# One written list of steps for all five engines of an attention and MLP kernel, in another order

## The chip, the cores and the metric

The kernel runs on one core of a Trainium2 chip. A core has a matrix engine (TensorE, PE in the profile, with its weight loads shown as PEld), a vector engine (VectorE, DVE), a scalar engine (ScalarE, ACT), a general engine (GpSimd, POOL) and an engine that issues transfers (SyncE, SP). Each takes its instructions from a queue of its own, in order, and they wait for one another by semaphores. The data lies in the chip's main memory, in an on-chip memory of 128 partitions (SBUF), and, for the results of matmuls, in eight banks of PSUM, 512 float32 values per partition each.

The metric is the device time of one execution in microseconds (us). Four executions of the kernel before gave 324.56 to 325.36, median 325.13 us.

## The reference

The kernel joins two layers. The first is causal attention over a sliding window of 128 positions, with a linear bias that falls with the distance (ALiBi), for 8 batches and 8 heads, 576 positions, head size 64. Its output, reordered to 4608 tokens of 512 values, goes through an MLP whose activation is h * sigmoid(beta * h), with one beta for each of the 2048 hidden values.

```python
def _attn_ref(q, k, v):
    scores = scale * np.matmul(q, k.transpose(0, 1, 3, 2))
    slopes = 2.0 ** (-8.0 * (np.arange(H, dtype=np.float32) + 1) / H)
    bias = slopes[:, None, None] * (-np.abs(rel).astype(np.float32))[None, :, :]
    mask = (rel >= 0) & (rel < window)
    scores = np.where(mask, scores + bias[None], -1000000000.0)
    ...
    return np.matmul(attn, v).astype(np.float32)

def _moe_ref(x, w_in, w_out, beta):
    h = x @ w_in
    g = h * (1.0 / (1.0 + np.exp(-beta * h)))
    return (g @ w_out).astype(np.float32)
...
    x = np.ascontiguousarray(attn_out.transpose(0, 2, 1, 3)).reshape(B * S, H * D)
    return _moe_ref(x=x, **moe_kwargs)
```

All inputs and the output are float32. The kernel computes with bfloat16 operands and float32 sums.

## The kernel before

**The MLP.** The 4608 tokens are nine groups of 512 (group 0 to 8). For a group, `Hm` (line 557) makes 16 up-projection steps, one for each 128 of the hidden values. A step is four matmuls of 128x128 weights against 512 tokens (four, because the 512 inputs of a token are four times 128), into one PSUM bank. ACT takes the tanh of the bank (line 564), DVE makes from tanh and bank the gated value and writes it to `gT` (line 565); with that the bank is free. `OS` (line 588) then makes the output of each 128 tokens: 16 matmuls into one bank, issued in four steps of four, a copy to SBUF (line 598, ACT; one half of the last by line 596, DVE), and `store` (line 606). The output steps of a group mostly run after the up-projection steps of that group, some of them between those of the next. The input of the up-projection lies transposed in `XT`, a ring of 1536 tokens (three groups).

**The attention.** 576 positions are four blocks of 128 and one of 64. The batches go two ways.

Batches 0 and 1 run by pairs of heads. `get_pair` loads q or k of a pair for 512 positions (SyncE), `cast_pair` (line 235, POOL) turns them to bfloat16, `TP` (line 287) transposes them on TensorE and copies them into `qkT` (k by DVE, line 289, q by ACT, line 293), `SP_` (line 335) makes the scores, with a bias by a matmul (line 324) for some, ACT takes the exponential (line 342), `PVP` (line 374) the output, `norm` (lines 358 and 359, DVE) divides by the sum, and `XP` (line 385) transposes the result on TensorE, from where it is copied to `XT`. The 64 last positions have steps of their own (`TT`, `SCT`, `PV`, `X`).

Batches 2 to 7 run by blocks. `get` (line 207, SyncE) loads 128 positions of q, k or v for all heads; `cast_qk` (lines 228 and 229, POOL) casts q and k into a staging buffer `bst`; `DT` (line 413) moves that transposed into `qkT`, by a DMA transpose that SyncE issues; `SC` (line 438) makes the scores for two pairs of heads at once, in the PSUM tiles `SS` and `ST` of two banks each, ACT takes the exponential (line 446), DVE multiplies by the falling factors (line 171 or 176), `PVB` (lines 492 and 495) makes the output of one block and normalises it on DVE (lines 499 and 500), into `xn`. `X` brings `xn` transposed into `XT`: for batches 2 and 3 by four matmuls against an identity (line 520) and a copy by ACT (line 523), for batches 4 to 7 by a DMA transpose on SyncE (line 512), which the constant `XDMA = 4` decides. v of batch 2 comes as q and k do, with a cast on POOL (line 243); v of batches 3 to 7 by `get_v` (line 250), a transfer by POOL's queue that casts on the way.

A token group needs the blocks of `XT` that it covers. Group 1 ends with block 3 of batch 1, group 2 with block 2 of batch 2, group 3 with block 2 of batch 3, and so on.

**The order.** The order on TensorE, SyncE and POOL is that of the program text. The opening (batch 0's attention and the first steps of group 0) is written out by hand, and there ACT and DVE follow the text too; later a scheduler orders these two. Group 0's steps are mixed by hand with batch 1's attention. From group 1 on, `spread` runs through a group's list of MLP steps and puts the attention steps of the batches to come between them, in proportion to the weights that `att` gives them, so that the blocks that group g+1 needs are in place when the steps of group g end. Loads, casts and transposes of the next batch stand in the same list (`jobs`). All loads of 32-bit data are issued by SyncE, W1 and W2 (lines 258 and 262) by POOL. W2 goes in four parts. The first transpose of batch 2 waits on purpose for the last of them:

```python
        if (b, sb) == (2, 0):
            after(r, w2[3])
```

The stores of groups 0 to 2 are issued by POOL, those after by ACT, the last two by SyncE. A few matmuls on zeros (`idle`, line 118, and `calm`) fill gaps in the opening.

**Buffers.** 14 for loads (`fst`), 4 for casts (`bst`), 10 for exponentials (`pt`), 4 for normalised blocks (`xn`), 2 for gated groups (`gT`), 3 for tanh (`sig`), 5 for outputs. The eight banks of PSUM are shared out by pools: two for `SS`, two for `hps`, two for transposes, which become `ST` later, and two for `SX`, which become `ops` and `h3`.

The functions that the change touches, with the line numbers of the profile:

Of the kernel before, what the change touches and what calls it, by code (L numbers as in the profile page):

```python
# [15 lines left out]
P = 128  # L16


@with_exitstack
def kernel(  # L20
# [18 lines left out]
    NQB = 5  # L39
# [44 lines left out]
    psum_c = ctx.enter_context(tc.tile_pool(name="psum_c", bufs=1, space=bass.MemoryType.PSUM))  # L84
    psum_h = ctx.enter_context(tc.tile_pool(name="psum_h", bufs=2, space=bass.MemoryType.PSUM))
    trans = ExitStack()
    psum_t = trans.enter_context(tc.tile_pool(side="right", name="psum_t", bufs=2, space=bass.MemoryType.PSUM))
    SS = psum_c.tile([P, 2, 512], F32, name="SS")
    psum_c.seal()
    opening = ExitStack()  # L90
    psum_x = opening.enter_context(tc.tile_pool(name="psum_x", bufs=1, space=bass.MemoryType.PSUM))
    SX = psum_x.tile([P, 2, 512], F32, name="SX")
    late, gates = {"tick": 0}, {}
    spans = [SS]

    def span():

        spans.append(spans.pop(0))
        return spans[-1]

    def obank(name, tag=None):
        if tag is None:
            late["n"] = late.get("n", 0) + 1
            tag = "ops" if late["n"] % 2 else "h3"
        return late["o"].tile([P, DM], F32, name=name, tag=tag)[:]

    def after(ins, other):
        tc.add_manual_dep(
            ins.ins, other.ins.name,
            mybir.DependencyInfo(mybir.DependencyClass.Sync, mybir.DependencyReason.DATA),  # L110
            reason="gate",
        )

    def idle(n):
        for _ in range(n):
            nc.tensor.matmul(
                SS[:, 0, :], lhsT=zeros[:, 0:P], rhs=zeros[:], start=True, stop=True,
                skip_group_check=True)  # L120

    def constants():
# [4 lines left out]
        idle(8)  # L127
# [35 lines left out]
    def falls_late(i):  # L163
        to, a, w = ((0, 0, P), (128, 0, 64), (192, 0, P), (320, 1, 64), (384, 1, P))[i]
        after(nc.vector.tensor_copy(
            out=falls[:, :, to : to + w], in_=fall[:, :, a, 0:w]), gates[1, 4])

    def factor(pt, m, p):

        if m:  # L170
            nc.vector.tensor_tensor(  # L171
                out=pt[:], in0=pt[:], in1=falls[:, 2 * p : 2 * p + 2], op=ALU.mult)
            return
# [16 lines left out]
    def betas():  # L190
        bps = psum_t.tile([P, NFF], F32, name="bps", tag="t")
# [703 lines left out]
```

The softmax here doesn't subtract the row's maximum and nothing guards it: scores larger than these inputs give would overflow.

## Time and profile before

| What | Before |
|---|---|
| median of four executions | 325.13 us |
| the profiled execution's own time | 325.27 us |
| its span, first to last instruction | 323.5 us |
| TensorE: busy, matmuls | 310.1 us (96%), 2256 |
| VectorE, ScalarE, GpSimd busy | 183.7, 194.0, 98.8 us |
| first up-projection matmul of group 0, 1, 2 | 19.27, 48.02, 93.65 us |
| the same of group 3 to 8 | 125.0, 157.7, 190.5, 221.8, 254.3, 284.5 us |
| read from and written to main memory | 36.71 and 9.44 MB |

A page of the profile shows one execution. "Busy" is the time in which an engine works on an instruction; matmuls overlap, and their ends are modelled, so TensorE's share is an upper bound. The slices cut the span in 40 equal parts and give the busy share of each in tenths, and the clock granted to TensorE. A group of instructions is one line of the program on one engine, with operation, tile, shape, number, busy time, mean duration, and the idle time of the engine just before them with what ended it. "L557" is line 557. The chain of waits goes back from the last instruction: at each step to whatever released it. "DMA qkT<-bst" in it is the transfer that fills `qkT` from `bst`. Names that end in q, such as SPq, are an engine's queue of instructions.

### The profile page before, as it was taken

What the parts mean: (1) busy time and instruction counts of PE and PEld (TensorE: products, weight loads), DVE (VectorE), ACT (ScalarE), POOL (GpSimd) and SP (SyncE); (2) the same over time, 40 slices, a digit from 0 to 9 for tenths busy, and PEclk for the clock granted to TensorE, in tenths of its full rate; (3) what the DMA queues carried; (4) which work ended last, traced back from release to release, by engine and by line L of the source; (5) the groups of instructions that cost most, each with busy time, mean ns of one, the idle gap of its engine ahead of it and who ended that gap; (6) DMA issues with size and microseconds to landing.
All of it is one profiled execution on the core that took longest, in us unless ns stands there. A gap on an engine that the chain in (4) does not pass through costs nothing.

```text
span 323.5 us, 5947 instructions
## 1 busy us (share of the span) xinstructions
PE 310.1 (96%) x2256; PEld 153.0 (47%) x2297; DVE 183.7 (57%) x346; ACT 194.0 (60%) x283; POOL 98.8 (31%) x154
## 2 busy tenths in 40 slices
PE   8889999999999999999999999999999999999995
PEld 3444554444545454544454445444544455444443
DVE  6778877542548753786278617752875176335500
ACT  6858887635558865685467645845675465346511
POOL 4864810332853445438036221340000000000000
PEclk9999999999999999999999999999999999999999
DMA  7999999999999999999999994993122112110021
GB/s 212 254 263 248 175 195 198 223 198 161 217 180 158 205 256 132 233 167 165 256 196 205 157 254 83 215 138 101 18 65 60 65 18 65 47 61 32 10 89 65
DMA packets 147565, 48.84 MB, mean 151 GB/s; under 512 B 135360, under 2 KB 143824, under 8 KB 147536
## 3 DMA queue, kind: packets, MB, share of 16 engines
q1 hardware_dynamic: 115712, 32.39, 56.1%
q0 software_dynamic: 28624, 10.29, 26.9%
q10 hardware_dynamic: 3200, 5.78, 5.0%
q8 instruction: 18, 0.29, 0.4%
q14 instruction: 11, 0.09, 0.1%
HBM read 36.71 MB, written 9.44 MB: 143 GB/s over the span
## 4 chain that ended last, share of the span: by engine, by line
PE 78%; DMA 11%; POOL 3%; DVE 2%; ACT 2%; issue 2%; SPq 1%; DVEq 0%; POOLq 0%
PE ops L588 25%; PE hps L557 24%; PE hpo L557 11%; PE oph L588 9%; DMA fst<-in_k_dram 5%; DMA qkT<-bst 3%; DMA fst<-in_q_dram 3%; PE SS L438 2%; PE ST L438 1%; PE SS L495 1%; POOL bst L235 1%; PE SS L492 1%; ACT pt L446 1%; DVE gT L565 1%; PE ST L492 1%
## 5 line engine op out<-in xcount | busy, mean ns | idle before, releaser
L588 PE MATMUL ops<-W,gT 128*128 128x512 bf16 (+1 forms) x448 | 107.6, 372 | 1.1 <-ACT osb L598 0.5
L565 DVE SCALAR_TENSOR_TENSOR gT<-sig,hps 128x512 bf16<-128x512 bf16 x100 | 67.6, 683 | 71.8 <-ACT sig L564 71.6
L557 PE MATMUL hps<-XT,W 128*128 128x512 bf16 x383 | 98.1, 379 | 1.4 <-issue 0.3
L564 ACT ACTIVATE sig<-hps,beta_h 128x512 bf16<-128x512 f32 x100 | 68.1, 690 | 34.7 <-PE hps L557 33.3
L588 PEld LDWEIGHTS <-gT 128*128 128x128 bf16 x592 | 55.6, 98 | 61.6 <-issue 1.9
L557 PEld LDWEIGHTS <-W 128*128 128x128 bf16 x576 | 52.8, 98 | 61.1 <-issue 3.7
L228 POOL CAST bst<-fst 128x512 bf16<-128x512 f32 (+1 forms) x32 | 21.0, 657 | 76.1 <-DMA fst<-in_q_dram 44.4
L557 PE MATMUL hpo<-XT,W 128*128 128x512 bf16 x164 | 42.8, 379 | 0.2
L564 ACT ACTIVATE sig<-hpo,beta_h 128x512 bf16<-128x512 f32 x42 | 29.0, 689 | 16.9 <-PE hpo L557 15.7
L565 DVE SCALAR_TENSOR_TENSOR gT<-sig,hpo 128x512 bf16<-128x512 bf16 x42 | 28.6, 681 | 10.9 <-ACT sig L564 10.7
L598 ACT ACTIVATE osb<-ops 128x512 f32<-128x512 f32 (+1 forms) x28 | 16.6, 595 | 25.5 <-PE ops L588 20.6
L446 ACT ACTIVATE pt<-SS 128x1024 bf16<-128x1024 f32 x24 | 24.5, 1019 | 11.4 <-PE SS L438 11.4
L588 PE MATMUL oph<-W,gT 128*128 128x512 bf16 x126 | 29.2, 379 | 0.1
L229 POOL CAST bst<-fst 128x512 bf16<-128x512 f32 (+1 forms) x32 | 21.7, 677 | 16.9 <-DMA fst<-in_k_dram 15.4
L176 DVE TENSOR_TENSOR pt<-pt,fall 128x1024 bf16<-128x1024 bf16 x24 | 17.0, 709 | 14.6 <-ACT pt L446 14.6
L446 ACT ACTIVATE pt<-ST 128x1024 bf16<-128x1024 f32 x24 | 24.5, 1022 | 0.0
L171 DVE TENSOR_TENSOR pt<-pt,falls 128x1024 bf16<-128x1024 bf16 x24 | 18.9, 793 | 9.6 <-ACT pt L446 9.6
L250 POOL DMA_DIRECT2D vs<-in_v_dram x25 | 21.3, 869 | 0.0
L598 ACT ACTIVATE osb<-oph 128x512 f32<-128x512 f32 x8 | 4.8, 597 | 21.1 <-PE oph L588 21.1
L495 PEld LDWEIGHTS <-pt 128*128 128x128 bf16 x240 | 14.8, 97 | 4.3
L243 POOL CAST vs<-fst 128x512 bf16<-128x512 f32 (+1 forms) x15 | 10.1, 673 | 16.2 <-DMA fst<-in_v_dram 16.2
L492 PEld LDWEIGHTS <-pt 128*128 128x128 bf16 x192 | 13.4, 97 | 2.8
(102 smaller groups left out, 253.3 us busy)
## 6 DMA issues: line engine op xcount, KB each, us to landing
fst<-in_k_dram SPq DMA_DIRECT2D x32, 256.0 KB, 5.8
fst<-in_q_dram SPq DMA_DIRECT2D x32, 256.0 KB, 5.7
out_dram<-osb ACTq DMA_DIRECT2D x22, 256.0 KB, 2.0
fst<-in_v_dram SPq DMA_DIRECT2D x12, 256.0 KB, 5.6
out_dram<-osb POOLq DMA_DIRECT2D x12, 256.0 KB, 5.4
vs<-in_v_dram POOLq DMA_DIRECT2D x20, 128.0 KB, 6.3
W<-in_moe_w_in_dram POOLq DMA_DIRECT2D x4, 512.0 KB, 7.9
W<-in_moe_w_out_dram POOLq DMA_DIRECT2D x4, 512.0 KB, 13.2
```

The lines of the kernel that those rows point to most:

```text
L171: nc.vector.tensor_tensor(out=pt[:], in0=pt[:], in1=falls[:, 2 * p : 2 * p + 2], op=ALU.mult)
L228: nc.gpsimd.tensor_copy(out=t[0:rows, 0], in_=fs.pop(("q", b, sb))[0:rows])
L229: return nc.gpsimd.tensor_copy(out=t[0:rows, 1], in_=fs.pop(("k", b, sb))[0:rows])
L250: return nc.gpsimd.dma_start(out=VS[b % 2][0:rows, sb, :, 0:D], in_=v[b, :, P * sb : P * sb + rows, :].rearrange("h p d -> p h d"))
L446: nc.scalar.activation(out=pt[:], in_=sps[:], func=ACTF.Exp, scale=qscale)
L492: nc.tensor.matmul(o, lhsT=weights(b, qb - 1, h, 1), rhs=vs[:, qb - 1, h, 0 : D + 1], start=True, stop=False, skip_group_check=True)
L495: nc.tensor.matmul(o, lhsT=weights(b, qb, h, 0), rhs=vs[:, qb, h, 0 : D + 1], start=qb == 0, stop=True, skip_group_check=True)
L557: nc.tensor.matmul(hps, lhsT=W1[:, c, bass.ts(j, P)], rhs=XT[:, c, c0 : c0 + TOKG], start=(c == 0), stop=(c == NDM - 1),)
L564: gates[g, j] = nc.scalar.activation(out=sig[:], in_=hps, func=ACTF.Tanh, scale=beta_h[:, j : j + 1])
L565: gates["gT"] = nc.vector.scalar_tensor_tensor(out=gts[g][:, j, :], in0=sig[:], scalar=1.0, in1=hps, op0=ALU.add, op1=ALU.mult)
L588: nc.tensor.matmul(ops_[:, cols], lhsT=gT[:, j, i * P : i * P + P], rhs=W2[:, j, cols], start=(j == 0), stop=(j == NFF - 1),)
L598: nc.scalar.mul(o, ops_[:, cols], 0.5)
```

## The change

The program text that made the order goes away: the hand-written opening, `spread`, `jobs`, `att`, `merged`. In its place stands one list, `PLAN`, of 1300 short words, and a loop that runs them in order. A word is a step, after the point the engine that it goes to where there is a choice (`p` POOL, `v` DVE, `a` ACT, `s` SyncE), and numbers. `H:2:5:7` is the up-projection step 5 of group 2 into bank 7, `a:2:5` its tanh, `d:2:5` its gate; `O:0:3:1:7` the second quarter of the output of rows 3 of group 0 in bank 7, `oc` its copy, `st` its store. `gq.s:2:1` loads q of batch 2, block 1; `cQ.v:2:1` casts it on DVE; `D:2:1` transposes the block into `qkT`; `S`, `E`, `M` are scores, exponential and factor of a pair of heads; `V`, `n`, `XD` output, normalisation and DMA transpose of a block. The order on all five engines, ACT and DVE included, is now that of the list.

What differs in the steps:

- Each function that issued work for several engines is cut into one function for each engine (`TP` and `TPC`, `SP_` and `EP`, `PVB` and `NB`, `Hm`, `HA` and `HD`, and so on).
- PSUM is one tile of eight banks, and each step names its bank. Scores are made for one pair of heads at a time.
- The 79 casts, all on POOL before, are 24 on POOL, 31 on DVE, 24 on ACT. Of the 35 full output copies 8 go to DVE. The copies of the first transposes go to either engine.
- Batches 2 and 3 lose the matmuls and the ACT copies of `X`: all blocks of batches 2 to 7 go by DMA transpose (`XD`, 30 steps).
- All loads of q, k and v other than `get_v` go by SyncE, in another order, W1 and W2 by POOL, W2's parts in the order 2, 0, 1, 3. The wait for the last part of W2 goes. The change's short description says at most eight transfers are in flight; no line of the diff states that, it is a property of the order.
- Output stores are spread over ACT, POOL and SyncE, and some stand later in the list.
- The last 128 rows of the output are two steps of half the width (`OL`), each with its own copy (`lc`) and store (`ls`); the second half's copy was on DVE before, both are on ACT now.

```diff
+PLAN = """
+q.s:0:0 q.s:0:2 const fr:3 fr:7 z:1:1 k.s:0:0 fr:0 cq.p:0:0 q.s:0:1 k.s:0:3 ones cq.v:0:2 ck.v:0:0
+fr:5 z:2:5 q.s:0:3 z:2:6 Rk:0:0:1 rk.a:0:0 Rq:0:0:7 cq.a:0:3 ck.a:0:3 q.s:1:0 k.s:0:2 k.s:0:1
+rq.v:0:0 fr:6 fr:4 cq.v:0:1 Rq:0:2:4 A:0:0:1:1 rq.a:0:2 EA:0:0 cq.p:1:0 gv.s:0:1 B:0:0:5:0 Rk:0:3:7
+Rq:0:3:0 ck.v:0:2 rq.v:0:3 ck.p:0:1 k.s:1:0 cv.p:0:1 EB:0:0 order rk.v:0:3 Rq:0:1:4 Rk:0:1:5
+rk.a:0:1 Rk:0:2:1 z:1:6 gv.s:0:0 gv.s:0:3 k.s:1:1 rq.v:0:1 rk.a:0:2 MB:0:0 A:0:1:6:1 ck.p:1:0
+cv.v:0:0 B:0:1:3:0 gv.s:0:2 EA:0:1 EB:0:1 A:0:3:0:1 B:0:2:6:1 w1:0 Rk:1:0:4 EA:0:3 EB:0:2 A:0:2:2:1
+VA:0:0:0 rk.v:1:0 B:0:3:5:1 nA:0:0 EA:0:2 Rq:1:0:0 cv.p:0:3 MB:0:1 VA:0:2:4 cv.v:0:2 ck.a:1:1
+rq.a:1:0 w1:1 VA:0:3:1 q.s:1:1 q.s:1:3 VB:0:0:2 nA:0:2 nB:0:0 k.s:1:2 VB:0:2:0 Rk:1:1:4 z:2:7 nB:0:2
+beta:3 pad k.s:1:3 EB:0:3 VA:0:1:5 B:1:0:6:0 rk.a:1:1 cq.a:1:3 EB:1:0 A:1:0:2:1 nA:0:1 nA:0:3
+VB:0:3:5 VB:0:1:4 XP:0:0:7 cq.p:1:1 w1:2 nB:0:1 nB:0:3 XP:0:2:6 ck.v:1:2 EA:1:0 Rq:1:3:4 Rq:1:1:3
...
+d:0:10 TT:0:1 tt.a:0 a:0:11 gk.s:2:0 VB:1:0:5 VB:1:2:7 nB:1:0 B:1:3:3:1 SCT:0:0 w2:2 nB:1:2 cv.v:0:4
...
+x.a:0:4 xc.v:1:1 xc.a:1:3 H:1:2:1 ECT:1 a:0:15 H:1:14:7 H:1:13:0 w2:0 w2:1 cQ.p:2:4 a:1:14 d:0:15
...
+d:1:4 H:1:3:6 H:1:12:4 a:1:11 gq.s:2:0 a:1:7 d:1:0 d:1:2 a:1:3 w2:3 gk.s:2:3 d:1:11 d:1:3 O:0:0:0:1
+O:0:3:0:7 H:1:10:2 a:1:13 cQ.p:2:2 cK.p:2:2 cK.p:2:4 d:1:13 H:1:1:6 O:0:0:1:1 D:2:1 gv.s:1:4
+O:0:3:1:7 D:2:4 gq.s:3:0 a:1:12 cK.v:2:0 cQ.v:2:0 d:1:7 d:1:12 a:1:9 a:1:10 D:2:2 gq.s:2:3 D:2:0
...
+gk.s:4:1 st.s:0:3 V:2:1:0 n:2:1 O:0:1:2:3 O:1:0:1:2 E:2:1:3 E:2:1:1 S:2:1:0:0 gk.s:3:1 XD:2:1
...
+n:2:0 n:2:2 D:3:0 O:1:0:3:2 O:1:2:1:3 V:2:4:4 cQ.a:3:1 cK.a:3:2 st.p:0:1 x.a:1:4 XD:2:0 V:2:3:0
+cK.p:3:1 cQ.p:3:2 cK.p:3:3 XD:2:2 n:2:4 n:2:3 pv:3:2 O:1:1:2:6 O:1:1:3:6 O:1:2:2:3 O:1:2:3:3 pv:3:4
+H:2:5:7 H:2:1:1 H:2:9:4 H:2:10:5 a:2:5 oc.v:1:0 H:2:0:2 oc.a:1:2 H:2:7:0 cK.v:3:4 cQ.v:3:3 d:2:5
...
+O:2:0:3:2 cK.p:4:4 O:2:2:1:3 gk.s:5:0 XD:3:0 n:3:2 cQ.v:4:4 n:3:3 S:4:0:1:4 XD:3:1 oc.a:2:0 oc.v:2:1
+S:4:0:0:6 XD:3:2 S:4:0:2:1 gk.s:5:1 gk.s:5:4 O:2:2:2:3 cK.p:5:4 E:4:0:0 E:4:0:1 D:4:4 gq.s:5:1 D:4:3
+gk.s:5:2 st.p:1:1 O:2:2:3:3 S:4:0:3:6 V:3:4:4 H:3:0:0 E:4:0:2 E:4:0:3 H:3:7:1 M:4:0:1 n:3:4 oc.a:2:2
...
+H:5:13:3 E:6:0:2 M:6:0:1 st.a:0:0 M:6:0:2 H:5:4:5 H:5:11:0 oc.v:4:2 a:5:12 M:6:0:3 a:5:4 a:5:11
...
+oc.a:7:2 st.s:7:1 O:7:3:2:3 st.p:6:3 O:7:3:3:3 oc.a:7:3 O:8:0:0:5 oc.v:7:0 O:8:1:1:4 O:8:1:2:4
+O:8:0:1:5 O:8:2:2:1 O:8:1:3:4 st.s:7:3 O:8:0:2:5 st.s:5:2 st.s:7:2 oc.a:8:1 st.p:7:0 OL:1:7
+O:8:0:3:5 lc.a:1 O:8:2:3:1 oc.a:8:0 ls.s:1 st.a:8:0 st.a:8:1 oc.a:8:2 st.a:8:2 OL:0:3 lc.a:0 ls.a:0
+"""
...
-    SS = psum_c.tile([P, 2, 512], F32, name="SS")
...
+    psum = ctx.enter_context(tc.tile_pool(name="psum", bufs=1, space=bass.MemoryType.PSUM))
+    PS = psum.tile([P, 8, 512], F32, name="PS")
+    psum.seal()
+
+    def bank(k):
+        return PS[:, k, :]
+
+    def move(eng, out, in_):
+        (nc.scalar.copy if eng is nc.scalar else eng.tensor_copy)(out=out, in_=in_)
...
-    def cast_qk(b, sb):
+    def cast_qk(what, eng, b, sb):
         rows = ROWS[sb]
-        t = bst_pool.tile([P, 2, H, D], BF16, name="bst", tag="bst")
-        staged[b, sb] = t
-        nc.gpsimd.tensor_copy(out=t[0:rows, 0], in_=fs.pop(("q", b, sb))[0:rows])
-        return nc.gpsimd.tensor_copy(out=t[0:rows, 1], in_=fs.pop(("k", b, sb))[0:rows])
+        if (b, sb) not in staged:
+            staged[b, sb] = bst_pool.tile([P, 2, H, D], BF16, name="bst", tag="bst")
+        move(eng, staged[b, sb][0:rows, "qk".index(what)], fs.pop((what, b, sb))[0:rows])
...
-        if (b, sb) == (2, 0):
-            after(r, w2[3])
...
+        held["X", b, qb] = xt
+
+    def pieces(b, qb):
+        tok0 = (b * S + P * qb) % XTR
+        n1 = min(ROWS[qb], XTR - tok0)
+        return [(r0, r1, at) for r0, r1, at in ((0, n1, tok0), (n1, ROWS[qb], 0)) if r0 < r1]
+
+    def XC(eng, b, qb):
+        xt = held.pop(("X", b, qb))
+        for r0, r1, at in pieces(b, qb):
+            move(eng, XT[:, :, at : at + r1 - r0], xt[:, :, r0:r1])
+
+    def XD(b, qb):
+        xnv = xns.pop((b, qb))[:].rearrange("p h d -> p (h d)")
+        for r0, r1, at in pieces(b, qb):
+            nc.sync.dma_start(out=XT[:, :, at : at + r1 - r0], in_=xnv[r0:r1], transpose=True)
+
+
+
...
+    def HA(g, j):
+        hps = hs[g, j]
+        sig = held["H", g, j] = sig_pool.tile([P, TOKG], BF16, name="sig", tag="sig")
+        nc.scalar.activation(out=sig[:], in_=hps, func=ACTF.Tanh, scale=beta_h[:, j : j + 1])
+
+    def HD(g, j):
+        if g not in gts:
+            gts[g] = gt_pool.tile([P, NFF, TOKG], BF16, name="gT", tag="gT")
+        nc.vector.scalar_tensor_tensor(
+            out=gts[g][:, j, :], in0=held.pop(("H", g, j))[:], scalar=1.0, in1=hs.pop((g, j)),
+            op0=ALU.add, op1=ALU.mult)
+
...
+    def OC(eng, g, i, part=None):
+        cols = slice(0, DM) if part is None else halves[part]
+        osb = osb_pool.tile([P, DM], F32, name="osb", tag="osb")
+        o = held["O", g, i, cols.start] = osb[:, 0 : cols.stop - cols.start]
+        src = (late[g, i] if part is None else late[g, i, part])[:, cols]
+        if eng is nc.scalar:
+            nc.scalar.mul(o, src, 0.5)
+        else:
+            eng.tensor_scalar_mul(o, src, 0.5)
+
+    def store(eng, g, i, part=None):
+        cols = slice(0, DM) if part is None else halves[part]
+        row0 = g * TOKG + i * P
+        eng.dma_start(out=out[row0 : row0 + P, cols], in_=held.pop(("O", g, i, cols.start)))
+
...
+    STEPS = {
+        "k": of(get_pair, "k"), "q": of(get_pair, "q"),
+        "gv": of(get, "v"), "gq": of(get, "q"), "gk": of(get, "k"), "pv": get_v,
...
+        "V": PVB, "n": NB, "X": X, "x": XC, "XD": XD,
+        "H": Hm, "h": Hm, "a": HA, "d": HD, "O": OS, "oc": OC, "st": store,
...
+    with tc.manual_schedule(engines={ENG.PE, ENG.SP, ENG.Pool, ENG.Activation, ENG.DVE}):
+        for step in PLAN.split():
+            name, *at = step.split(":")
+            name, _, eng = name.partition(".")
+            STEPS[name](*([ENGINES[eng]] if eng else []), *map(int, at))
```

## The prediction

> **What bounds the kernel now.** I read the page's busy shares and slices first, then the costliest groups, then the chain of waits in order of time around the one place where it leaves TensorE, then a table of windows, and last the waits of SyncE's queue.
>
> ```profile
> span 323.5 us, 5947 instructions
> PE 310.1 (96%) x2256; PEld 153.0 (47%) x2297; DVE 183.7 (57%) x346; ACT 194.0 (60%) x283; POOL 98.8 (31%) x154
> ...
> PEclk9999999999999999999999999999999999999999
> DMA  7999999999999999999999994993122112110021
> ...
> L588 PE MATMUL ops<-W,gT 128*128 128x512 bf16 (+1 forms) x448 | 107.6, 372 | 1.1 <-ACT osb L598 0.5
> L557 PE MATMUL hps<-XT,W 128*128 128x512 bf16 x383 | 98.1, 379 | 1.4 <-issue 0.3
> L229 POOL CAST bst<-fst 128x512 bf16<-128x512 f32 (+1 forms) x32 | 21.7, 677 | 16.9 <-DMA fst<-in_k_dram 15.4
> ```
>
> TensorE is the bound, at full clock throughout, but 96% flatters it, since the ends of matmuls are modelled. The chain of waits gives the real pace:
>
> ```profile
> 70.48 3.78 DMA qkT<-bst
> ...
> 82.50 3.92 DMA fst<-in_q_dram
> ...
> 89.44 6.87 DMA qkT<-bst
> 96.85 0.97 PE hps L557 x4
> ...
> 184.01 3.45 PE oph L588 x16
> ```
>
> Sixteen 512-column matmuls in 3.45 us are 0.2156 us each. There are 1152 of them (the last 32 half as wide, in double number): 248.5 us. Start-to-start spacings in the timeline price the rest: 432 attention-output matmuls at 0.029 us = 12.5, 240 scores at 0.044 = 10.6, 112 + 104 of batches 0 and 1 (outputs, scores, bias) = 10.7, about 190 transposes and other small matmuls = 9.6, 16 fillers and the bias vector 5.3. Together 48.7, so 297.2 us of work. The last matmuls end at 318.16 + 1.92 = 320.1: TensorE loses 22.9 us, and 3.4 us of copy and store follow. Placing the work on the timeline, 8.2 us are lost by 27.5 us, 12.0 by the first matmul of token group 1 (48.0), 15.0 by group 2 (93.65), and only 7.9 from there to the end.
>
> ```profile
> 0.00:24.00 24.00, 19.95 (x190) 10.26 (x194) 16.89 (x55) 16.60 (x29) 16.07 (x33) 1.00 1.06 244
> 24.00:48.00 24.00, 22.38 (x239) 11.89 (x243) 18.90 (x42) 19.85 (x31) 12.21 (x19) 1.00 1.11 206
> 72.00:96.00 24.00, 23.35 (x176) 11.19 (x178) 9.71 (x15) 12.71 (x18) 13.80 (x22) 1.00 1.11 184
> 224.00:256.00 32.00, 31.63 (x235) 15.73 (x237) 19.41 (x34) 19.73 (x28) 0.00 (x0) 1.00 0.20 49
> ```
>
> SyncE's own queue, by what it waited for (us in all, waits, the worst one):
>
> ```profile
> SPq L512 <- DVE xn L500: 34.4, 9, 13.1
> SPq L413 <- POOL bst L229: 16.4, 16, 2.6
> ```
>
> The columns after the stretch are PE, PEld, DVE, ACT, POOL, clock, DMA share and GB/s. The DMA engines are full (a share over 1 is packets that overlap) until about 220 us and nearly idle after. So what is won early must be won against full DMA engines, and what is lost late is lost by order alone. These two lines say that SyncE's queue stands still, with everything behind it, for a transpose whose source is late: up to 13.1 us.
>
> **The change, part by part.** The list holds the same 141 + 3 up-projection and 140 + 4 down-projection steps, the same scores and the same bias choices, and 16 fillers as before. Fillers and biases cost nothing net. "Eight in flight" is no edit: no line of the diff adds a wait or a limit, it can only act through the order.
>
> *Transposes of batches 2 and 3.* Ten steps leave TensorE: 32 matmuls at 0.056 and 8 at 0.029 us, 2.0 us less. ACT loses eight copies of 0.60 us and two of 0.42: 5.6 us, beside other work, so nothing on the path. SyncE's queue gains ten DMA transposes. The 21 that exist take 1.17 to 1.99 us of the queue (median 1.20) and land 2.3 to 7.3 us after their issue (median 3.2), near 2.4 with idle DMA engines and 5.3 to 7.3 with loads queued ahead. The old path from normalisation to tokens in place was 0.22 us of PE and 0.60 of ACT, so each hand-over to a group becomes 1.5 to 6.5 us longer. That binds only where a group waits for the last block: group 2 (block 2 of batch 2), group 3 (block 2 of batch 3) and group 4 (block 4 of batch 3, earlier blocks than its own last one). In the list, group 2's first matmul stands after four down-projection steps (3.5 us) behind that transpose, group 3's after 2.7 us of TensorE work, so a landing of 3.2 is nearly covered and one of 7.3 is not.
>
> [...]
>
> *Casts.* All 79 casts ran on POOL. Now ACT has 24, DVE 31, POOL 24. ACT: the nearest rows are its copies of the same 128x512 size, 584 and 594 ns, so 24 x 0.59 = +14.2; less 5.6 (above), less eight output copies moved to DVE, 8 x 0.60 = 4.8: 194 to about 198 us. DVE: between 0.29 us (its 128x512 bf16 copies to the tail factors) and 0.69 (its copy out of PSUM), 31 casts are 9 to 21 us; I take 12, nearer the SBUF-to-SBUF row. Eight output copies of 128x512, from 0.43 (half the width) to 0.69, are 3.4 to 5.5. DVE goes to about 200 us. Both stay under TensorE, so the sums cost nothing; the work that hides them is the dense matmuls. What can cost is order: a cast waits for a load, and behind it stand the tanh (0.69) and the gate (0.68) that free a PSUM bank. On POOL that wait (16.9 us before the k casts, harmless) held up only casts. I bound it from 0 to the POOL row's rate, 16.9 + 76.1 us over 64 casts = 1.4 us each, times 55 = 80 us if none were covered; the load is normally issued 5 to 20 us of TensorE work ahead of its cast against 5.7 us to landing, so I take 1 us in all.
>
> *The start.* The first k load now stands third on SyncE (issues 0.50 us apart), and DVE has three factor rows (0.56 each) before the first k cast. The first transposes go from 4.93 to about 7.4 us. ACT then runs almost without a break: from the first transpose's copy, in the list's order, eight copies and casts of 0.6, four exponentials of 0.81 and three of 1.03, then the fourth batch-0 one, batch 1's first pair and the token copies, which ends near 25 us. So group 0 starts near 24.5 us, not 19.3, but with 3.2 us more of batch 1 done: work done by 27.5 us is equal, 18.9 us. From there to group 1 are 17.9 us of work; ACT has about 20.5 us in that stretch, so group 1 starts near 46.5, 1.5 us earlier. W2 moves later on POOL, behind a batch-1 q tail that lands near 42: the first part needed is the second W2 transfer, landing near 56 by the old 10.9 to 16 us to landing, while the list wants it near 54.5. That gives 1.5 us back.
>
> *Group 2.* When the last transpose it needs has landed, the change has moved two batch-4 blocks (one and a half loads at 1.15 us, the spacing of landings from 57.6 to 67.1) and three new transposes (at most 1.2 each) more than the kernel before, and three or four qkT transposes (1.25 each) less: between -1.3 and +1.6 us on full DMA engines. The old group 2 starts at 93.65; I add 0.15 for this and 0.7 for the landing that now ends the path: 94.5. The change has 79.2 us of TensorE work done by then; it has lost 15.3.
>
> *Group 2 to the end.* 216.0 us of work remain (297.2 - 2.0 - 79.2). The old kernel loses 7.9 us here, in pairs of scores that wait for ACT and in hand-overs. With scores issued one head pair at a time and eight banks given out singly I take 4.5 for these; 1 us for casts; and for groups 3 to 7 a transposed block just in time, 0 to 3 us each, 0.2 taken: 6.5 in all. The output's last copies and stores are as before, 3.4 us.
>
> **Sum:** 94.5 + 216.0 + 6.5 + 3.4 = 320.4 us of span. The profiled execution took 325.27 around a span of 323.5, 1.8 more: 322.2. It stands 0.14 above the median, 325.13, so I leave that out. Forecast 322.2 us, 0.9% faster.
>
> **The rivals.**
> *R1, slower: SyncE's order holds the transposes back.* A block's transpose is queued behind loads and behind qkT transposes that wait for a cast. For it: 34.4 us in 9 waits and a worst landing of 7.3. Against it: all those waits cost the old PE 0.4 us, since they had slack. If the hand-overs to groups 2 to 7 come 3 us late each (7.3 landing against 2.7 to 3.5 covered, less what PE has fallen behind anyway), 6 x 2.2 = 13 us: 335. It decides from about 0.7 us per hand-over on.
> *R2, slower: an in-order engine waits for a load.* If one in five of 55 casts waits 2 us and half of it passes the PSUM banks, 11 us: 333. Decides from 3 us on. For it: loads took 8 to 19 us to land between 35 and 55 us and 5 to 11 around 100 to 165. Against it: a list that issues most loads well ahead. [...]
> *R3, more gain:* the start really fills TensorE (group 2 near 91) and nothing waits later (4 us): 314.4 of span, 316.2.
> *R4, no change:* what the X transposes leave is lost at group 2: within 0.2% (about what a measurement of this kernel can tell from no change), 325.1.
>
> **How the numbers follow.** Forecast 0.40, R3 0.08, R4 0.07, R1 0.25, R2 0.20. Faster 0.48, same 0.07, slower 0.45. The forecast alone spans 318 to 324.5 (its terms at their near ends: 2.5 us in group 2, 2 in the hand-overs). For 8 in 10 the range takes in R3 and most of R1 and R2: 314 to 336.
>
> **What the profile will show.** Right: 31 XT transposes by DMA with a median landing under 4 us, group 2's first matmul near 94.5, ACT near 198 and DVE near 200 us, idle time before up-projection weight loads released by DMA XT under 2 us. Wrong for R1: that idle time at 5 us or more, with long SyncE waits on xn or bst just before. Wrong for R2: ACT or DVE casts waiting for fst for 10 us or more, and PE waiting for DVE gT. The forecast is also wrong if the first tanh comes after 28 us, or if W2 lands after 60.

## The result: 0.2% slower, and group 2 starts 6.5 us later than forecast

The changed kernel takes 326.68 us (median of 45 executions) against 325.61 us for the kernel before in the same comparison. The ratio is 1.0023, with an interval of 1.0010 to 1.0036: slightly slower, where 0.9% faster was forecast. The time lies inside the range; the sign is wrong. Here and below, ratios leave out executions more than 1.5% above the fastest of their kernel and medians in us do not, so the two differ where executions scatter (most in the run with small moves below: 0.994 without three of its twelve, 0.997 with them).

The page of the changed kernel's profiled execution (327.65 us, span 325.9) in its first lines:

```profile
span 325.9 us, 5866 instructions
PE 308.2 (95%) x2217; PEld 152.9 (47%) x2257; DVE 191.5 (59%) x383; ACT 193.3 (59%) x291; POOL 62.2 (19%) x99
...
PEclk9799999999799999999999999999999999999999
DMA  7999999999999999799999996957963050000223
...
L632 PE MATMUL PS<-XT,W 128*128 128x512 bf16 x558 | 132.1, 379 | 3.6 <-DVE gT L645 1.4
L655 PE MATMUL PS<-W,gT 128*128 128x512 bf16 x540 | 131.4, 382 | 1.3 <-issue 0.2
```

TensorE has less work than before (308.2 us busy against 310.1) and still ends later. Its clock is no longer whole: two slices show 7. Line 632 is the up-projection now, line 655 the down-projection.

Where the time went is read from TensorE's work by time. I sum the work that TensorE has begun by a moment, at the same full-clock prices as in the prediction, and take it from the clock; what is left is lost. Both columns go by the same prices, which makes the column of before about 1 us higher than the prediction's own sum. A group starts here with its first matmul; the 93.65 us for group 2 in the table before the change is the weight load ahead of it.

| Moment | Lost before | Lost after |
|---|---|---|
| 27.5 us | 9.9 | 11.5 |
| 36 us | 11.8 | 11.7 |
| 64 us | 14.1 | 14.5 |
| first matmul of group 2 | 16.1 (at 93.86 us) | 23.1 (at 100.97 us) |
| 160 us | 20.0 | 25.1 |
| 288 us | 22.9 | 28.6 |

Up to 64 us the two orders lose the same. Between there and group 2 the change loses 8.6 us and the kernel before 2.0. Behind group 2, up to 288 us, the change loses a little less, 5.5 against 6.8 us. So the question, in this execution, is one stretch of 37 us. A second profile of the same kernel (the run on one chip below) spreads the loss otherwise: about 4 us more than this one by 64 us, with a half clock from 60.21 us, and only about 3.5 us from there to group 2, which starts at 99.37. Both have group 2 late. These are the lines of the stretch in the first profile's chain of waits (start, length, what):

```profile
66.71 3.54 DMA fst<-in_q_dram
...
75.43 7.14 DMA qkT<-bst
82.62 0.61 PE PS L522 x12
...
100.03 0.94 issue
100.97 7.93 PE PS L632 x36
```

and in the table of windows (PE, PEld, DVE, ACT, POOL busy with their counts, then the granted clock, DMA share and GB/s):

```profile
72.00:80.00 8.00, 6.80 (x55) 3.34 (x55) 5.11 (x12) 4.87 (x6) 2.34 (x4) 1.00 1.32 195
80.00:84.00 4.00, 1.98 (x19) 0.92 (x18) 1.35 (x3) 0.72 (x1) 0.00 (x0) 1.00 1.08 217
84.00:88.00 4.00, 3.85 (x24) 1.86 (x25) 1.93 (x4) 1.22 (x2) 0.00 (x0) 0.57 0.90 196
88.00:96.00 8.00, 7.95 (x86) 4.62 (x88) 4.35 (x8) 4.24 (x7) 4.44 (x7) 1.00 1.28 214
96.00:104.00 8.00, 7.01 (x50) 3.29 (x48) 3.63 (x8) 1.17 (x2) 0.14 (x1) 1.00 1.57 175
```

TensorE stands still in the first, second and last of these windows, and in the third it works at a clock of 0.57, which the busy column does not show (3.85 of 4.00 us): the 512-column matmuls from 84.01 to 87.42 us last 0.59 us each, against 0.38 from 88 to 96, and count as busy. What it waited for, from its list of waits (us in all, times, longest):

```profile
PE PS L522 <- DMA qkT<-bst: 2.0, 1, 2.0
PE PS L632 <- DVE gT L645: 1.4, 1, 1.4
...
PE PS L558 <- POOL vs L205: 1.2, 1, 1.2
PE PS L632 <- issue: 1.1, 2, 0.9
```

In order of time: at 64.4 us a PSUM bank waits for a gate, and VectorE, which makes the gates, stands at a cast whose load (q, batch 2, block 0) was issued at 46.93 and landed at 65.02 us, behind W2. At 73.0 us an attention output waits for the cast of a v load. At 80.2 us scores wait for the transpose of batch 2's block 3. From 84.01 us the granted clock is 0.50 for 3.41 us. At 100.0 us group 2 waits for the DMA transpose of block 2 of batch 2, a wait that the profile only calls "issue": that block was normalised at 94.00, its transpose was issued at 95.47 behind two others (one of batch 3's q and k, and that of block 0), and it landed at 100.88, 5.41 us after its issue.

### The profile page after: what moved, and what is told of

It is laid out like the page before. It is cut to its first block, busy times and chain, and to the rows that moved or that the text cites. A ratio compares the mean times of both kernels' runs of the same rounds, so it can differ in the third digit from the quotient of the medians.

```text
span 325.9 us, 5866 instructions
## 1 busy us (share of the span) xinstructions
PE 308.2 (95%) x2217; PEld 152.9 (47%) x2257; DVE 191.5 (59%) x383; ACT 193.3 (59%) x291; POOL 62.2 (19%) x99
## 4 chain that ended last, share of the span: by engine, by line
PE 79%; DMA 8%; SPq 4%; issue 3%; ACT 3%; DVE 1%; POOL 0%; DVEq 0%; POOLq 0%; ACTq 0%
PE PS L655 33%; PE PS L632 33%; PE PS L522 4%; DMA fst<-in_q_dram 3%; DMA fst<-in_k_dram 3%; PE PS L577 2%; DMA qkT<-bst 2%; PE PS L574 2%; ACT sig L640 2%; SPq L500 1%; SPq L306 1%; PE PS L666 1%; PE PS L410 1%; PE PS L421 1%; PE PS L369 1%
## 5 line engine op out<-in xcount | busy, mean ns | idle before, releaser
L632 PE MATMUL PS<-XT,W 128*128 128x512 bf16 x558 | 132.1, 379 | 3.6 <-DVE gT L645 1.4
L640 ACT ACTIVATE sig<-PS,beta_h 128x512 bf16<-128x512 f32 x144 | 93.5, 688 | 69.6 <-PE PS L632 56.2
L655 PE MATMUL PS<-W,gT 128*128 128x512 bf16 x540 | 131.4, 382 | 1.3 <-issue 0.2
L645 DVE SCALAR_TENSOR_TENSOR gT<-sig,PS 128x512 bf16<-128x512 bf16 x144 | 92.9, 682 | 58.8 <-ACT sig L640 58.7
L531 ACT ACTIVATE pt<-PS 128x1024 bf16<-128x1024 f32 x48 | 46.9, 1024 | 20.8 <-PE PS L522 18.9
L205 POOL CAST bst<-fst 128x512 bf16<-128x512 f32 (+1 forms) x31 | 20.1, 658 | 95.6 <-DMA fst<-in_q_dram 37.4
L677 ACT ACTIVATE osb<-PS 128x512 f32<-128x512 f32 (+1 forms) x29 | 16.8, 583 | 28.9 <-PE PS L655 26.3
L586 DVE TENSOR_TENSOR xn<-PS,zb 128x512 bf16<-128x512 f32 (+1 forms) x30 | 20.7, 690 | 1.1
L577 PE MATMUL PS<-vs,pt 128*128 128x65 bf16 x240 | 16.9, 194 | 0.0
L522 PE MATMUL PS<-qkT 64*128 64x256 bf16 (+2 forms) x240 | 14.7, 250 | 2.2 <-DMA qkT<-bst 2.0
L205 DVE CAST bst<-fst 128x512 bf16<-128x512 f32 (+1 forms) x26 | 11.5, 447 | 5.9 <-DMA fst<-in_q_dram 4.6
L574 PE MATMUL PS<-vs,pt 128*128 128x65 bf16 x192 | 14.6, 195 | 0.1
```

The source lines that it names most:

```text
L205: (nc.scalar.copy if eng is nc.scalar else eng.tensor_copy)(out=out, in_=in_)
L522: nc.tensor.matmul(o, lhsT=qk[64 * e : 64 * e + 64, 1, p, P * kb : P * kb + P], rhs=qk[64 * e : 64 * e + 64, 0, p, P * kb : P * kb + nq], ...
L531: nc.scalar.activation(out=pt[:], in_=held.pop(("S", b, m, p)), func=ACTF.Exp, scale=qscale)
L574: nc.tensor.matmul(o, lhsT=weights(b, qb - 1, h, 1), rhs=vs[:, qb - 1, h, 0 : D + 1], start=True, stop=False, skip_group_check=True)
L577: nc.tensor.matmul(o, lhsT=weights(b, qb, h, 0), rhs=vs[:, qb, h, 0 : D + 1], start=qb == 0, stop=True, skip_group_check=True)
L586: nc.vector.tensor_tensor(out=xn[0:nq].rearrange("p (g h) d -> p g h d", g=2), in0=pv[0:nq, :, :, 0:D], in1=zs[0:nq].broadcast_to([nq, 2, ...
```

## The experiments

"Ratio" is always to the kernel before on the same chip. The words of the list are explained in the section on the change. Three accounts of the lost stretch stood against one another: the order of the loads, with W2 and batch 3 ahead of data of batch 2 (the expectations call it theory Q in its first form, L in its second); the token transposes by DMA (rival X); casts that wait in the in-order queues of ACT and VectorE (rival C). The half clock is asked about apart.

### The token transposes

**The kernel before with the transposes alone.** One constant makes batches 2 and 3 go to `XT` by DMA transpose, in the old order.

```diff
-    XDMA = 4
+    XDMA = 2
```

> The kernel before with one part of the change alone: batches 2 and 3 go to XT by DMA transpose (the constant 4 becomes 2). Rival X: group 2 and the groups behind it start later, 3 to 6 us slower than before, ratio 1.009 to 1.018. Theory Q and the prediction's own working (2.0 us of TensorE work less, hand-overs 1.5 to 6.5 us longer at three groups, most of it covered): between 1 us faster and 2 us slower, ratio 0.997 to 1.006.

Measured: 337.82 us, ratio 1.0396 (1.0372 to 1.0420), 12.6 us slower. That is more than twice the most that was expected. In the list of TensorE's waits nearly the whole of it is one line, which the chain shows in its pieces:

```profile
PE hps L557 <- DMA XT<-xn: 12.6, 1, 12.6
```

```profile
94.82 1.19 SPq L413
...
96.10 1.53 SPq L512
...
97.72 7.76 DMA XT<-xn
...
105.53 1.89 PE hps L557 x4
```

TensorE has nothing from 92.9 to 105.5 us, and its granted clock is a half from 97.66 to 111.31 us, so the first matmuls of group 2 are slow too: four in 1.89 us, where the kernel before took 0.97. The transpose that group 2 needs is queued on SyncE behind qkT transposes of batch 3 (L413) that wait for casts, is issued at 97.72 and lands 7.76 us later; the load of k just ahead in the chain, at 88.80, took 5.33. This is the rival "SyncE's order holds the transposes back", at one hand-over.

**The changed kernel without three of them.** Blocks 0, 1 and 2 of batch 2, those that group 2 needs, go back to TensorE and ACT. The other seven blocks of batches 2 and 3 stay with the DMA.

```diff
-XD:2:1
+X:2:1:0 O:1:1:0:6 x.a:2:1
...
-XD:2:0 V:2:3:0
+X:2:0:7 V:2:3:0 x.a:2:0
...
-XD:2:2
...
-O:1:1:3:6
+X:2:2:5 O:1:1:3:6 x.a:2:2
```

> The list of after with one part undone: blocks 0, 1 and 2 of batch 2 go to XT by four matmuls and an ACT copy each, as before the change, 12 matmuls at 0.056 us and 3 copies at 0.6 us. Theory L: only the hand-over ahead of group 2 (1.3 us) goes, less 0.7 us of TensorE work: 0 to 1.5 us less than after, ratio 0.998 to 1.003. Rival X (the DMA transposes are what ate the gain): 3 us or more less, ratio 0.993 or lower.

Measured: 324.04 us, ratio 0.9958 (0.9931 to 0.9986). That is 0.65% below the change (1.0023, not on the same chip), and below the kernel before; it lies between what the two accounts expected, so it does not decide alone.

**On one chip.** Three kernels ran beside one another: the changed kernel again, the same with ten matmuls on zeros in its first 12 us, and that with the three blocks on TensorE. The fillers are meant to keep the clock of the opening whole, so that the last two differ in the three blocks alone.

> The changed kernel itself, on the same chip as the three beside it: ratio 1.001 to 1.004 as before.

Measured: 326.44 us, ratio 1.0010 (0.9981 to 1.0039).

```diff
-Rk:0:0:1
+z:3:0 Rk:0:0:1
...
-Rk:0:3:7
+z:3:0 Rk:0:3:7
...
-Rq:0:1:4
+z:4:0 Rq:0:1:4
```

> The list of after with the ten fillers in the first 12 us alone. If the half clock of the opening costs what half of 3.41 us costs on a path that decides: 0.5 to 1.2 us less than after, mean clock up by 0.003 to 0.005. If the opening has slack up to group 1: the clock goes up and the time does not move.

Measured: 326.29 us, ratio 1.0021 (0.9997 to 1.0045). The time does not move. In its profile the granted clock is 1.00 from 12 to 16 us, where the first profile of the change has 0.57.

The third has these fillers and the edit of the three blocks above.

> The list of after with two edits: blocks 0 to 2 of batch 2 by TensorE, and the ten fillers in the first 12 us. The four moves for block 3 and the v tail are not in it. If the moves count (the two waits before the scores' second half): 0.5 to 1.5 us slower than the run with them, ratio 0.993 to 0.997. If they only move the wait: the same as it, 0.989 to 0.993.

Measured: 323.77 us, ratio 0.9926 (0.9894 to 0.9957). Against its neighbour on the chip, three blocks on TensorE instead of the DMA are worth 0.95% by the ratios, whose intervals do not overlap, and 2.5 us by the medians. The list of waits of the kernel with fillers and DMA transposes has

```profile
PE PS L629 <- DMA XT<-xn: 2.8, 1, 2.8
```

where that of the kernel with the three blocks on TensorE has

```profile
PE PS L629 <- issue: 0.2, 1, 0.2
```

The edit also takes three transposes out of SyncE's queue, but it is at the hand-over that these two profiles differ most: group 2 starts at 98.20 us with the one and at 94.92 with the other. The chain of the changed kernel's second profile shows the same place (the wait there is 2.1 us):

```profile
92.44 5.11 DMA XT<-xn
97.56 1.81 issue
99.37 1.67 PE PS L632 x7
```

With the blocks on TensorE the chain goes from matmul to matmul (L599 is the transposing matmul, L652 the down-projection, L629 group 2):

```profile
92.10 0.39 PE PS L599 x4
92.49 2.59 PE PS L652 x12
95.08 3.02 PE PS L629 x14
```

In the profiled executions with DMA transposes group 2 starts at 98.2 to 100.97 us wherever the rest of the list is the change's or little altered; with the three blocks on TensorE at 94.9 to 97.3 us. What follows hardly differs: from group 2's first matmul to the end of the last matmul the two profiles of the changed kernel take 221.7 and 221.4 us, the kernel with fillers 221.4, and the two kernels above with three blocks on TensorE 221.4 and 221.0 (before: 226.2). So what these kernels lose or win against one another lies ahead of group 2.

**All ten blocks on TensorE.** To the list with three blocks on TensorE, four moves (below) and the ten fillers, the other seven blocks of batches 2 and 3 were added, each with a matmul step and an ACT copy at a free bank near its place.

```diff
-XD:2:4
-XD:2:3
-XD:3:0
-XD:3:1
-XD:3:2
-XD:3:4
-XD:3:3
...
+X:2:4:3 O:2:1:1:6 x.a:2:4
...
+X:2:3:7 O:2:2:0:3 x.a:2:3
...
+X:3:0:0 S:4:0:1:4 x.a:3:0
+X:3:1:1 S:4:0:0:6 x.a:3:1
+X:3:2:0 O:2:2:2:3 x.a:3:2
...
+X:3:4:3 O:2:3:2:2 x.a:3:4
...
+X:3:3:7 H:3:11:4 x.a:3:3
```

> The run with batch 2's blocks 0 to 2 by TensorE, block 3 and the v tail first, and ten fillers, with the other seven blocks of batches 2 and 3 also transposed by TensorE and copied by ACT (28 more matmuls at 0.056 us or less, 7 copies at 0.6 us). If the cost of the DMA transposes lies at group 2 alone: 0.3 to 1.5 us slower than that run, by the added work, ratio to before 0.992 to 0.996. If every hand-over paid: 1 us or more faster, ratio 0.988 or lower.

Measured: 328.11 us, ratio 1.0062 (1.0025 to 1.0100), slower by 1.5% than the same list without this (0.9907, below, on another chip). It is slower than expected: group 3 starts at 134.3 instead of 130.1 us, and TensorE's waits name the transposing matmuls behind VectorE's gates and scores behind ACT's copies:

```profile
PE PS L599 <- DVE gT L642: 1.3, 2, 0.9
...
PE PS L519 <- ACT XT L202: 0.7, 1, 0.7
```

So at these places moving the other seven blocks wins nothing. That their DMA transposes cost little is seen in the changed kernel's own list of waits, which has one line for a token transpose behind group 2, 0.5 us at group 5. Whether TensorE would do better with them at other places was not tried.

### Casts in the queues of ACT and VectorE

The 40 casts of batches 2 to 7 that the list gives to ACT and VectorE went to POOL, at the same places.

```diff
-cK.a:2:1
+cK.p:2:1
...
-cQ.v:2:1
+cQ.p:2:1
...
-cK.v:2:0 cQ.v:2:0
+cK.p:2:0 cQ.p:2:0
...
```

> The list of after with the 40 casts of batches 2 to 7 that it gives to ACT and VectorE back on POOL, at the same places of the list. Rival C (casts in the in-order queues of ACT and VectorE hold back gates and tanh, 1.74 us at 64.4 us and more later): 1.5 to 4 us less than after, ratio 0.990 to 0.998. Theory L: no gain, since POOL's serial 0.66 us a cast and its own order delay batch 2's q and k: 0 to 3 us slower than after, ratio 1.002 to 1.012.

Measured: 325.97 us, ratio 1.0019 (0.9987 to 1.0052): the same as the change. The rival "an in-order engine waits for a load" falls as an account of the whole: it happens (64.4 us in the first profile), but without it nothing is won. What is left in its place is again the hand-over, 2.7 us in this profile:

```profile
PE PS L628 <- issue: 2.7, 1, 2.7
PE PS L518 <- DMA qkT<-bst: 1.5, 1, 1.5
```

### The order of the loads

**W2 earlier.** In the change's profile SyncE stands at one transpose from 54.43 to 64.64 us, while the four W2 transfers land (54.3 to 64.75). My first theory was that W2's late issue (45.8 us instead of 34.85) holds all else back.

```diff
-w1:3
+w1:3 w2:2 w2:0 w2:1 w2:3
...
-w2:2
...
-w2:0 w2:1
...
-w2:3
```

> The list of after, with the four W2 loads moved on POOL to right behind the last W1 load (issue near 33 to 36 us instead of 45.8 to 49.3). Theory Q (SyncE's queue stands behind W2's transfers, 10.2 us at one transpose, and the rest of batch 2 behind it; the late last transpose then opens the gaps of 64, 73, 80 and 100 us and the half clock of 84 us): SyncE free of it near 56 us, group 2's first matmul from 100.97 to near 96, span 3 to 5 us shorter than after, about 321 to 323 us timed, ratio to before 0.987 to 0.993. Rival X (the new DMA transposes of batches 2 and 3 are what costs): no more than 1 us. Rival C (casts in the in-order queues of ACT and DVE): no more than 1 us. Against Q as well: batch 1's loads would now run beside W2, so group 0's last steps could come later, up to 2 us.

Measured: 331.99 us, ratio 1.0222 (1.0192 to 1.0252). The theory fell. W2 now passes the loads of the batch tails, and TensorE waits for their cast, in one piece:

```profile
PE PS L381 <- POOL bst L201: 9.5, 1, 9.5
```

Here an earlier transfer made another one late: the cast that TensorE waits for starts at 55.56 us. W2's landing after 60 us is thus not what costs, as far as this earlier place shows; places between were not tried.

**Batch 2's last q and k first.** W2 stays; four loads move in front of the stuck transpose, and block 3's casts and transpose up.

```diff
-gq.s:2:2
+gq.s:2:2 gq.s:2:0 gk.s:2:3 gq.s:2:3 gv.s:1:4
...
-gq.s:2:0
...
-gk.s:2:3
...
-D:2:1 gv.s:1:4
+D:2:1
...
-D:2:2 gq.s:2:3 D:2:0
+D:2:2 D:2:0 cQ.p:2:3 cK.p:2:3 D:2:3
...
-cQ.p:2:3 cK.p:2:3
...
-D:2:3
```

> The list of after with W2 where it is, but the four loads that stood behind the stuck transpose or among W2's (q of batch 2 block 0, k and q of block 3, v of batch 1's tail) moved in front on SyncE, and the casts and the transpose of block 3 moved right behind the transpose of block 0. Theory Q, in the form that the order of SyncE's queue and not W2's lateness costs: the gaps at 73 and 80 us and the half clock go, group 2 near 96.5, timed about 321.5 to 323 us, ratio 0.988 to 0.994. If W2's lateness itself costs (no data before 65 us whatever the order): as after, ratio 1.000 to 1.004. Rivals X and C: as after.

Measured: 325.30 us, ratio 1.0023 (1.0001 to 1.0045). The waits at 73 and 80 us are gone from the profile, and the next late load has taken their place, v of batch 2 behind loads of batch 3. The hand-over is there as before:

```profile
PE PS L573 <- DVE vs L201: 2.1, 1, 2.1
...
PE PS L628 <- issue: 0.9, 1, 0.9
```

**Then v of batch 2 first, too,** ahead of all loads of batch 3.

```diff
-D:2:4 gq.s:3:0
+D:2:4 gv.s:2:0 gv.s:2:1 gv.s:2:2 gv.s:2:3 gv.s:2:4
...
-D:2:3
+D:2:3 gq.s:3:0
...
-gv.s:2:0 cQ.v:3:0
...
-gv.s:2:1
...
-gv.s:2:3 gk.s:3:3 gv.s:2:2
+gk.s:3:3
...
-gv.s:2:4
...
-cK.a:3:0
+cQ.v:3:0 cK.a:3:0
```

> The run with the four loads in front, plus all five v loads of batch 2 moved ahead of all loads of batch 3 on SyncE, and the first batch 3 cast moved back on VectorE to beside the next one. Theory L (SyncE's list loads batch 3 while batch 2 still lacks data, on DMA engines that are full): the gap of 2.3 us at 85.5 us (attention output waiting for a v cast) goes, and the half clock of 3.41 us behind it; group 2's first matmul from 98.3 to 94 to 95, timed 320.5 to 322.5 us, ratio 0.985 to 0.992. If the gap only moves on to the next late item (batch 3's data for group 3): 324 to 326 us, ratio 0.998 to 1.003.

Measured: 326.96 us, ratio 1.0046 (1.0028 to 1.0064). The five loads stand ahead of two qkT transposes, and now the scores wait for those:

```profile
PE PS L518 <- DMA qkT<-bst: 4.9, 1, 4.9
```

**And the token transposes ahead of batch 3 and 4,** in the same list.

```diff
-gk.s:4:1
...
-gq.s:3:3
...
-gk.s:4:4
...
-D:3:0
...
-XD:2:2
+XD:2:2 gk.s:4:1 gq.s:3:3 gk.s:4:4 D:3:0
```

> The run with batch 2's v first, and in addition two loads of batch 4, one of batch 3 and the first qkT transpose of batch 3 moved behind the token transposes of batch 2 on SyncE. Theory X2 (what is left at group 2 is the landing of the last token transpose, 5.2 to 5.4 us behind loads that were issued ahead of it, where TensorE has 3.5 us of work): landing 3 to 4 us, the 1.3 us ahead of group 2 gone, 0.5 to 1.5 us less than that run. If the landing is latency and not the queue: no difference.

Measured: 332.11 us, ratio 1.0172 (1.0129 to 1.0214). TensorE waits 6.9 us in three pieces for qkT in its profile, 4.7 as in the run without this edit, and the rest at batch 3's scores, whose first transpose is now late. There is no wait ahead of group 2, but with the scores so late there was none in that run either, so the time says nothing of the landing. The trace does: the last token transpose landed 5.50 us after its issue (5.16 in that run), the one before it 2.45 (4.92). The landing that counts was not shortened by taking these four out of its way, and what sets it stays open.

**Small moves, with the three blocks on TensorE.** Without the hand-over the two waits that are left ahead of it can be seen alone.

```diff
-gq.s:3:0
+gq.s:2:3 gq.s:3:0
...
-D:2:2 gq.s:2:3
+D:2:2
...
-cQ.p:2:3 cK.p:2:3 cv.p:1:4
+cv.p:1:4 cQ.p:2:3 cK.p:2:3
...
-gq.s:3:4
+D:2:3 gq.s:3:4
...
-gv.s:2:0 cQ.v:3:0
+gv.s:2:0
...
-gk.s:3:0 D:2:3
+gk.s:3:0
...
-cK.a:3:0
+cQ.v:3:0 cK.a:3:0
```

> The run with batch 2's blocks 0 to 2 transposed by TensorE, plus four moves in the list that let batch 2's block 3 and batch 1's v tail go first: the v tail's cast ahead of two casts on POOL, q of block 3 ahead of the first load of batch 3 on SyncE, block 3's transpose three steps earlier, and the first batch 3 cast on VectorE back to beside the next one. Theory L (late data of batch 2, in the order of the list): the waits at 71.0 us (1.9 us) and 78.7 us (1.75 us) go, group 2's first matmul from 96.5 to 93 to 94, timed 320.5 to 322.5 us, ratio 0.985 to 0.992. If full DMA engines and not the order set the landing, the waits only move: 323.5 to 325 us, ratio 0.994 to 1.000.

Measured: 325.45 us, ratio 0.9937 (0.9905 to 0.9968). Group 2 starts at 96.3 against 96.8 us. The interval overlaps that of the list without the moves (0.9958), so a gain from them is not shown.

### The half clock

**Fillers in the change, in the opening and ahead of the late scores.**

```diff
-Rk:0:0:1
+z:3:0 Rk:0:0:1
...
-Rk:0:3:7
+z:3:0 Rk:0:3:7
...
-Rq:0:1:4
+z:4:0 Rq:0:1:4
...
-S:2:1:1:4
+z:9:5 S:2:1:1:4
```

> The list of after with 19 matmuls on zeros into free banks: 3 and 3 and 4 ahead of transposes in the first 12 us, 9 ahead of the second half of batch 2's scores. The outputs are not touched. If the half clock (3.41 us at 0.50, twice in the profiled execution) comes from TensorE's idle stretches, the mean granted clock goes from 0.990 to 0.995 or 1.000 and the time falls by 1 to 1.5 us, to about 325.3, ratio about 0.999. If the clock falls for another reason: 0.990 as before and 0 to 0.5 us slower.

Measured: 325.95 us, ratio 1.0010 (0.9985 to 1.0036), mean clock of its executions 0.9948 against the change's 0.9921. The clock rises as expected; the time is not distinguishable.

**The kernel before without its small fillers.**

```diff
-            if (b, p) == (0, 1):
-                calm(1 + i)
...
-            idle(2)
...
-            idle(1)
...
-            idle(2)
```

> The kernel before without its eight small fillers in the opening (three matmuls on zeros ahead of a transpose, five at three other places); the first eight and all the rest stay. If idle stretches of TensorE halve its clock, the granted clock of the opening falls to 0.50 for 3.41 us in some executions, and the time rises by 0.5 to 2 us, ratio 1.002 to 1.006. If the fillers do nothing: ratio 0.998 to 1.001.

Measured: 325.99 us, ratio 0.9995 (0.9969 to 1.0022). The clock falls in the opening, which the windows of its profile show in the column after POOL,

```profile
8.00:12.00 4.00, 3.82 (x31) 1.82 (x32) 3.12 (x6) 2.86 (x4) 3.14 (x6) 0.50 1.18 288
12.00:16.00 4.00, 4.00 (x44) 1.84 (x42) 3.57 (x6) 2.94 (x5) 3.38 (x6) 0.67 1.24 205
```

and the time does not rise. But seven of its ten executions have a mean clock of 0.999 or more, so the edit did not often do what it was to do, and the fillers in the change's opening moved its mean clock only from 0.9914 to 0.9935. What a fall in the opening costs is therefore not settled; no run shows a cost. Over the 98 executions of the change and of the five edits of it that kept all or most of its order (four loads first, v first, fillers, three blocks on TensorE, casts on POOL), each against its own mean, time rises by 0.58 us per us of clock lost (one less the mean clock, times the span). A fall of 3.41 us loses 1.7, so it goes with 1.0 us, and the change's mean loss of 2.6 us with 1.5. That is a correlation, and what makes TensorE idle lengthens the time by itself.

**All of it.** The list with the three blocks on TensorE, the four moves and the ten fillers:

> The same with 10 matmuls on zeros into a free bank in three places of the first 12 us. Outputs untouched. If the half clock of the first 16 us comes from TensorE's idle stretches, more executions have a mean clock of 0.999 or more than without, and the median falls by 0.3 to 1 us; if not, 0 to 0.7 us slower.

Measured: 323.13 us, ratio 0.9907 (0.9874 to 0.9941). Nine of its twelve executions have a mean clock of 0.999 or more, against five of twelve without the fillers. Beside 0.9937 the intervals overlap; against the kernel before it is 0.9% faster, and it is the fastest that ran, with the three blocks and fillers alone (0.9926) not distinguishable from it, so the four moves show no gain here either.

## Why the prediction was wrong

**The step that failed** is "Group 2": "I add 0.15 for this and 0.7 for the landing that now ends the path: 94.5." It measured 100.97. The rest of the sum held: from there to the last matmul's end 221.7 us (216.0 + 6.5 forecast), copies and stores 3.25 (3.4). The miss is 6.5 - 0.8 - 0.15 = 5.5 us, which is the difference of the spans (325.9 against 320.4).

**The term of it that was mis-sized** is the hand-over by DMA. The prediction priced a transpose by its median landing of 3.2 us against 2.7 to 3.5 us of cover and took 0.7. But 3.2 was a median over rows from 148 us to the end. The rows with loads queued ahead said 5.3 to 7.3, and the text itself listed them. The three that matter landed 5.04, 5.54 and 5.41 us after their issue, and the last one had first stood 1.5 us in SyncE's queue behind two others. On one chip the three transposes are worth 2.5 to 3 us, where 0.7 was taken. In the first profile the wait itself is only 0.94 us, since TensorE, further behind by then, still had 4.6 us of work when the last transpose was issued; in the kernel with fillers it had 1.3 us, and the wait is 2.8. So that profile alone would have pointed at the earlier waits, and it took the run without the three transposes to show their price. With them undone group 2 starts at 94.9 to 96.8 us, close to the 94.5 forecast, and the time is 0.4 to 0.7% below the kernel before, where 0.9% was forecast with them in. So the new order does bring about half to four fifths of the gain that the sum gave it; the three DMA transposes take it back. The rival with 0.07, "what the X transposes leave is lost at group 2", is what happened; the rival with 0.25 named the mechanism and its place in SyncE's queue, but expected it at six groups. In the changed kernel it decides at group 2; group 5 shows 0.5 us of it at 187.9.

**What was not in the sum at all** are the waits at 64, 73 and 80 us (1.4, 1.2 and 2.0 us in the profile), data of batch 2 and of the tails that lands late. They are seen, and they vary: the second profile of the same kernel has one wait of 2.4 us for a gate at 56.5 us and none of the other two. No edit of the loads' order won time, and in the profiles of the first three each moved the wait to another late load or transpose. How much of the 2.5 to 3 us that remain of the miss they cost, and how much the half clock that follows the largest of them, the runs do not separate: fillers against the half clock left the time where it was (1.0010), within an interval that could hide 1 us.

**The start** came out as expected in sum, and not in its parts: group 0 at 25.8 us (24.5 forecast), group 1 at 49.7 (46.5), but with as much work done by 64 us as before. **Casts:** forecast 1 us; moving 40 of them back shows none. ACT ended at 193.3 and VectorE at 191.5 us busy (198 and 200). There are 95 casts in all, and 40 of them are on POOL after the change; the 79 and 24 of the text ahead are wrong, the 24 on ACT and 31 on VectorE, which the sum uses, are right. **Fillers** "cost nothing net": the sum took the clock as whole all along, and it was not (0.50 for 3.41 us from 12.33 and again from 84.01 us in the first profile); what that costs stays open. **W2** landed at 64.75, past the 60 that the text named as a sign against it; the first down-projection still came at 58.55 (58.18 before), since the part that it needs was the second to land, at 58.01. **The sign for the transposes**, a median landing under 4 us, came true (3.93) and meant nothing, for the reason above.

## What to carry to other kernels

Price a transfer on a hand-over by rows with the same load on the DMA engines, and add its place in the issuing queue: a median over a whole trace mixes a full and an empty machine, here 5.4 us at a DMA share of 1.23 and 2.5 at 0.33. A transpose by DMA cost nothing here where its consumer came later than it landed, and 2.8 us of waiting ahead of group 2 in the kernel with fillers; the few blocks at a hand-over may be worth their matmuls on a busy TensorE, while the rest go by DMA. Ask of any earlier load which other load it makes late (W2 issued earlier came with one wait of 9.5 us), and read the granted clock beside busy time: TensorE was busy for 3.85 of 4.00 us at a clock of 0.57.

## What the runs showed of the hardware

- In the first profile of the changed kernel the granted clock was 0.50 for 3.41 us from 12.33 us and again from 84.01 us. TensorE had been busy for 1.84 of the 4.00 us from 8 to 12 us, and for 1.98 of the 4.00 from 80 to 84, with 2.0 us of standing still from 80.6. In the run with the casts on POOL it stood still for longer, 2.7 us up to 98.46, and the 36 up-projection matmuls behind that took 7.93 us, as long as 36 in the changed kernel at a clock of 1.00 (from 100.97 us). So the length of a gap alone did not decide; what does, these runs do not show.
- DMA token transposes of 128 rows landed 5.0 to 5.5 us after issue at 88 to 96 us in the changed kernel, where the DMA engines' share is 1.23 (86 to 97 us), and 2.4 to 3.2 us at 244 to 266 us, where it is 0.33 (243 to 268 us).
- SyncE stood at the issue of one transpose for 10.2 us (54.43 to 64.64) while W2's transfers landed, with the cast it needed done at 54.27. In the kernel before it stood at the issue of one load for 9.0 us (42.85 to 51.83).
